# Third spectral stage of a fused spectral and gated kernel: spectrum as weights, the matrix over s1 streamed

## The chip, the cores and the metric

One core of one Trainium2 chip. The metric is device time in microseconds of one execution of the whole kernel. Three runs of the kernel before gave a median of 1438.85 us (1438.41 to 1439.46).

## What is computed

The reference, cut to what matters: one layer norm, then a sum of the input, a two-dimensional spectral filter and a gated block of two layers.

```python
B, S, D, F = 1, 2048, 576, 4608

def _A_ref(x, w_r, w_i):
    X = jnp.fft.rfft2(x, axes=(-2, -1))
    X = X * (w_r + 1j * w_i)
    return jnp.fft.irfft2(X, s=(S, D), axes=(-2, -1))

def _B_ref(x, w_gate, w_up, w_down):
    g = x @ w_gate
    u = x @ w_up
    return (sigmoid(g) * u) @ w_down

xn = layernorm(A_x)
out = A_x + _A_ref(xn, w_r, w_i) + _B_ref(xn, w_gate, w_up, w_down)
```

All numbers are float32. Matrix products run in float32r; where the precision asks for it an operand is split into a high part (rounded by a copy to float32r) and a low part (the difference), and a product becomes three: high by high, low by high, high by low.

## The kernel before

**The gated block** fills most of the time. The 2048 rows are taken in two halves (`PAIRS`), the inner dimension F in 36 blocks `f`; a unit `u` (function `unit`, helper `prod`, line 644) multiplies one block in seven block products of seven 128 x 512 matmuls each. These are the runs `pA`, `pB`, `pE` of seven matmuls. The way down is `down` (`po`, line 751) and, in the second half, `seven` (`ps`, line 842), which yields six matmuls of 288 columns for each pair of PSUM banks, and lets VectorE add each pair to `acc` or `qs` (line 852).

**The spectral filter** is computed beside the second half of the gated block. Rows are written as s = 32 s1 + s2; a product over s1 (64 values, real and imaginary parts stacked to 128) and one over s2 make the transform over the rows, and a matrix product over the 576 columns (folded to 288 by symmetry) makes the one over the columns. Three stages:

- `phase1b` (16 tiles): columns, then s1; its result goes to `sc1` in DRAM.
- `phase2` (16 blocks): s2, the multiplication by the filter, and s2 back (`pc`); the result `u`, two slices of 128 x 290, goes to `sc2` in DRAM with one copy by ScalarE (line 548) and one DMA.
- `phase3` (16 tiles): loads two slices of 128 x 290 from `sc2`, and the matrix over s1 `ai` (its high and low part for both slices); splits the spectrum into `uh` and `ul`; multiplies with `ai` as weights and the spectrum streamed (`py`, line 573, six matmuls of 290 columns); copies 256 of the 289 columns to `y` and splits the 33 left over into `rp` (high, low, high again); transposes both through TensorE (`pz`, lines 585 and 588, six transposes); splits the transposed result into `z3h`, `z3l` and the left-over rows `z3r`; multiplies by the matrix over the columns `dit` (`pe`, line 602, 14 matmuls of 288 columns); and adds the result to `acc` or to a spilled part of it (`fin`).

The spectral columns stand in the order of `KOF`: 256 columns, then 33 more (`FR` = 33, `REM` = 32), then one of zeros, which makes `NQ` = 290.

**The order of the work.** Each phase is a generator, started at a step of the main loop (`U1`, `U2`, `U3`: first step and steps between tiles; phase 3 starts at step 151 and every 4.5 steps). A step is one run of seven 512-column matmuls, then one piece of `seven` or `down`, then one piece (up to the next `yield`) of every active generator. Instructions of one engine run in the order in which the tile framework puts them; its scheduler may move a piece by some instructions, save those held by `keep_in_program_order`. All PSUM pairs (`pair`: `ps`, `po`, `py`, `pz`, `pe`, `pc` and others) share two buffers, so that each waits for the readers of the pair before the last. DMAs are issued by SyncE (SP) in one queue, with few exceptions at start and end. The rooms of the stages (`stage2`, `stage3`) hold the tiles of one stage each.

`split` writes the high part on ScalarE and the low part on VectorE:

```python
def split(hi, lo, src, eng=None):
    nc.scalar.activation(hi, src, AF.Copy)
    (eng or nc.vector).tensor_tensor(lo, src, f32(hi), op=OP.subtract)
```

Of the kernel before, what the change touches and what calls it, by code (L numbers as in the profile page):

```python
# [9 lines left out]
F32 = mybir.dt.float32  # L10
F32R = mybir.dt.float32r
I32 = mybir.dt.int32
AF = mybir.ActivationFunctionType
OP = mybir.AluOpType
PSUM = bass.MemoryType.PSUM

P = 128
S, D, F = 2048, 576, 4608
KD = D // 2 + 1
NQ = KD + 1  # L20
N1, N2 = 64, 32
NT = S // P
EPS = 1e-5
HD = D // 2
FR = HD + 1 - 2 * P
CW = 512
TPC = CW // P
PAIRS = S // (2 * CW)
TPP = 2 * TPC
KT = 2  # L30
REM = HD - KT * P
# [32 lines left out]
def _constants():  # L64
    out = {}

    mid = np.arange(HD) - (D - 1) / 2
    ang = 2 * np.pi * mid[:, None] * KOF[None, :] / D
    t = np.zeros((P, 2, 5, NQ), np.float32)
    for e, v in ((0, np.cos(ang)), (1, -np.sin(ang))):  # L70
        m = np.zeros((HD, NQ))
        m[:, :KD] = v
        m[:, KD - 1 if e == 0 else KT * P] = 0.0
        hi, lo = _split(m)
        for part, w in ((0, hi), (1, lo)):
            t[:, e, 2 * part] = w[:P]
            t[:, e, 2 * part + 1] = w[P:2 * P]
        t[:KR, e, 4] = np.concatenate([hi[2 * P:], hi[2 * P:], lo[2 * P:]])
    out["cf"] = t.reshape(P, 10 * NQ)


    s1 = np.arange(N1)
    k1 = np.arange(N1)
    am = np.zeros((P, N2, 2, P), np.float32)
    ai = np.zeros((P, N2, 2, P), np.float32)
    for s2 in range(N2):
        ph = 2 * np.pi * (((N2 * s1[:, None] + s2) * k1[None, :]) % S) / S
        m = _cplx(np.exp(-1j * ph))
        am[:, s2, 0], am[:, s2, 1] = _split(m)
        m = _cplx(np.exp(1j * ph).T)  # L90
        ai[:, s2, 0], ai[:, s2, 1] = _split(m)
    out["am"] = am.reshape(P, N2 * 2 * P)
    out["ai"] = ai.reshape(P, N2 * 2 * P)


    s2 = np.arange(N2)
    ph = 2 * np.pi * ((s2[:, None] * s2[None, :]) % N2) / N2
    bm = _cplx(np.kron(np.exp(-1j * ph), np.eye(2)))
    bi = _cplx(np.kron(np.exp(1j * ph), np.eye(2)))
    sca = np.arange(P).reshape(2, N2, 2).transpose(1, 0, 2).ravel()  # L100
    bm = bm[sca]
    bi = bi[:, sca]
    b = np.stack([*_split(bm), *_split(bi)], 1)
    out["bm"] = b.reshape(P, 4 * P)


    a = np.where((KOF == 0) | (KOF == HD), 1.0, 2.0)[:, None] / (D * S)
    co, si = a * np.cos(ang.T), a * np.sin(ang.T)
    co[KD - 1] = 0.0
    si[KT * P] = 0.0  # L110
    t = np.zeros((P, 2, 5, HD), np.float32)
    for e, m in ((0, co), (1, si)):
        hi, lo = _split(m)
        for part, w in ((0, hi), (1, lo)):
            t[:, e, 2 * part] = w[:P]
            t[:, e, 2 * part + 1] = w[P:2 * P]
        t[:3 * FR, e, 4] = np.concatenate([hi[2 * P:], hi[2 * P:], lo[2 * P:]])
    out["di"] = t.reshape(P, 10 * HD)
    out["id"] = np.eye(P, dtype=np.float32)
    return out  # L120
# [25 lines left out]
def spectral_glu_kernel(ctx: ExitStack, tc: tile.TileContext, x, ri, w_in, w_down, out):  # L146
    nc = tc.nc
    con = {k: nc.inline_tensor(v, name=f"c_{k}").ap() for k, v in _constants().items()}

    def f32(ap):  # L150
        return ap.bitcast(F32)
# [6 lines left out]
    def pair(name):  # L158
        return ps.tile([P, 2, 512], F32, tag="pp", name=name, bufs=2)

    fix = ctx.enter_context(tc.tile_pool(name="fix", bufs=1))
    idf = fix.tile([P, P], F32, name="idf")
    idr = fix.tile([P, P], F32R, name="idr")
# [15 lines left out]


    sc1 = tc.dram_tile([N2 * P, NQ], F32, name="sc1")
    sc2 = tc.dram_tile([N2 * P, NQ], F32, name="sc2")
    spill = tc.dram_tile([TPP * P, D], F32, name="spill")
    wsp = [tc.dram_tile([P, NX * 5 * P], F32, name=f"wsp{f}") for f in range(NF)]
    wdsp = [tc.dram_tile([P, 2 * D], F32, name=f"wdsp{f}") for f in range(NF)]
# [17 lines left out]
# [3 lines that stand above are left out]
# [305 lines left out]
    def phase2(i):  # L511
        pool, bm, zz = R["pool"], R["bm"], R["zz"]
        kl = 2 * i
        x2 = pool.tile([P, 2, NQ], F32, tag="x2", name=f"x2{i}", bufs=2)
        nc.sync.dma_start(x2, sc1.rearrange("(p kl) n -> p kl n", kl=N2)[:, kl:kl + 2])
        w = pool.tile([P, 2, 2, KD], F32, tag="ri", name=f"ri{i}", bufs=2)
        nc.sync.dma_start(w.rearrange("p a j n -> p (a j n)"), ri[i])
        wr, wi = w[:, 0], w[:, 1]
        yield
        yield  # L520
        yield
        h = pool.tile([P, 2, NQ], F32R, tag="x2h", name=f"x2h{i}")
        l = pool.tile([P, 2, NQ], F32R, tag="x2l", name=f"x2l{i}")
        tc.keep_in_program_order(nc.scalar.activation(h, x2, AF.Copy))
        nc.vector.tensor_tensor(l, x2, f32(h), op=OP.subtract)
        yield
        pb = pair(f"pb{i}")
        for j in range(2):
            for n, (k, m) in enumerate(((0, h), (0, l), (1, h))):
                nc.tensor.matmul(pb[:, j, :NQ], bm[:, k, :], m[:, j, :], start=n == 0, stop=n == 2)  # L530
        sw = pool.tile([P, 2, KD], F32, tag="sw", name=f"sw{i}")
        nc.scalar.activation(sw[:N1], pb[N1:, :, :KD], AF.Copy, scale=-1.0)
        nc.scalar.activation(sw[N1:], pb[:N1, :, :KD], AF.Copy)
        z = pool.tile([P, 2, KD], F32, tag="z", name=f"z{i}")
        t2 = pool.tile([P, 2, KD], F32, tag="t2", name=f"t2{i}")
        nc.vector.tensor_tensor(z, wr, pb[:, :, :KD], op=OP.mult)
        nc.vector.tensor_tensor(t2, wi, sw, op=OP.mult)
        nc.vector.tensor_tensor(z, z, t2, op=OP.add)
        zh, zl = zz[i % len(zz)]
        split(zh[:, :, :KD], zl[:, :, :KD], z)  # L540
        yield
        yield
        pc = pair(f"pc{i}")
        for j in range(2):
            for n, (k, m) in enumerate(((2, zh), (2, zl), (3, zh))):
                nc.tensor.matmul(pc[:, j, :NQ], bm[:, k, :], m[:, j, :], start=n == 0, stop=n == 2)  # L546
        u = pool.tile([P, 2, NQ], F32, tag="u", name=f"u{i}", bufs=2)
        nc.scalar.activation(u, pc[:, :, :NQ], AF.Copy)
        nc.sync.dma_start(sc2.rearrange("(p kl) n -> p kl n", kl=N2)[:, kl:kl + 2], u)

    def phase3(t):
        pool, di = R["pool"], R["di"]
        u = pool.tile([P, 2, NQ], F32, tag="u3", name=f"u3{t}", bufs=2)
        nc.sync.dma_start(u, sc2[2 * t * P:(2 * t + 2) * P].rearrange("(j p) n -> p j n", j=2))
        ai = pool.tile([P, 2, 2, P], F32R, tag="ai", name=f"ai{t}", bufs=2)
        load_r(ai, con["ai"][:, t * 4 * P:(t + 1) * 4 * P].rearrange("p (a h m) -> p a h m", a=2, h=2))
        if t < TPP:
            a = pool.tile([P, D], F32, tag="fin", name=f"fin{t}", bufs=2)
            nc.sync.dma_start(a, spill[t * P:(t + 1) * P, :])
        else:  # L560
            a = acc[t]
        yield
        yield
        yield
        uh = pool.tile([P, 2, NQ], F32R, tag="uh", name=f"uh{t}")
        ul = pool.tile([P, 2, NQ], F32R, tag="ul", name=f"ul{t}")
        tc.keep_in_program_order(nc.scalar.activation(uh, u, AF.Copy))
        nc.vector.tensor_tensor(ul, u, f32(uh), op=OP.subtract)
        yield
        py = pair(f"py{t}")  # L570
        for sl in range(2):
            for n, (h, m) in enumerate(((0, uh), (0, ul), (1, uh))):
                nc.tensor.matmul(py[:, sl, :NQ], ai[:, sl, h, :], m[:, sl, :], start=n == 0, stop=n == 2)  # L573
        y = pool.tile([P, 2, 2 * P], F32, tag="y", name=f"y{t}")
        nc.scalar.activation(y, py[:, :, :2 * P], AF.Copy)
        rp = pool.tile([P, 2, 3, FR], F32R, tag="rp3", name=f"rp3{t}")
        rem = py[:, :, 2 * P:KD]
        split(rp[:, :, 0, :], rp[:, :, 1, :], rem)
        nc.scalar.activation(rp[:, :, 2, :], rem, AF.Copy)
        yield  # L580
        pz = pair(f"pz{t}")
        for k in range(2):
            v = pz[:, 0, k * 256:(k + 1) * 256].rearrange("p (c a s) -> p c a s", c=2, a=2)
            for sl in range(2):
                nc.tensor.transpose(v[:, :, sl, :], y[:, sl, k * P:(k + 1) * P], idf)  # L585
        v = pz[:3 * FR, 1, :256].rearrange("p (c a s) -> p c a s", c=2, a=2)
        for sl in range(2):
            nc.tensor.transpose(v[:, :, sl, :].bitcast(F32R), rp[:, sl].rearrange("p a b -> p (a b)"), idr)
        zh = pool.tile([P, 2, 2, P], F32R, tag="z3h", name=f"z3h{t}")
        zl = pool.tile([P, 2, 2, P], F32R, tag="z3l", name=f"z3l{t}")  # L590
        zr = pool.tile([P, 2, P], F32R, tag="z3r", name=f"z3r{t}")
        split(zh, zl, pz[:, 0, :].rearrange("p (a c s) -> p a c s", a=2, c=2))
        nc.scalar.activation(zr[:3 * FR], pz[:3 * FR, 1, :256].rearrange("p (c s) -> p c s", c=2), AF.Copy)
        yield
        pe = pair(f"pe{t}")
        for e in range(2):
# [8 lines left out]
        lo, up = a[:, :HD], a[:, HD:]  # L605
# [414 lines left out]
    for p in range(PAIRS):  # L1020

        calls = [(0, 0), (1, 0), (0, 1), (1, 1)] if p == 0 else [(0, 0), (0, 1), (1, 0), (1, 1)]
        for n, (f, c) in enumerate(calls):
            u = p * NF + f
# [34 lines left out]
        for f in range(G, NF):  # L1059
            u = p * NF + f  # L1060
# [79 lines left out]
```

## Time and profile before

| | us |
|---|---|
| median of 3 runs | 1438.85 |
| profiled execution | 1438.32 |
| its span, first to last instruction | 1436.5 |
| third spectral stage, first `py` to last `pe` | 1184 to 1410 |
| second spectral stage | 960 to 1160 |

How to read the profile: PE is TensorE's matmuls, PEld its weight loads (which overlap matmuls), DVE is VectorE, ACT ScalarE, SP SyncE. Matmuls are pipelined and the ends of their records are modelled: the time that one occupies is read from start to start, or from the chain of work that ended last. That chain follows the work back from the last instruction, at each step to what released it or to the instruction before it on its engine; its pieces give start, length, and the number of instructions. A group of instructions has its line, engine, operation, output and inputs, shape (for a matmul: rows x weight columns, then rows x streamed columns), count, busy time, the mean of one in ns, and the engine's idle time before it with what ended it.

### The profile page before, as it was taken

Reading aid. Unit: us, or ns where it says so; the run is one execution under the profiler, and the core shown is the slowest. Engines: PE = TensorE matmul, PEld = TensorE weight load, DVE = VectorE, ACT = ScalarE, POOL = GpSimd, SP = SyncE. Lnnn points to the kernel's source line nnn. Section 1 sums busy time; section 2 is a strip of 40 time slices with the busy share of each in tenths; the row PEclk is TensorE's granted clock in tenths of the full one; section 3 lists DMA queues with packets and bytes.
Section 4 is the critical chain, followed back from the end, with each engine's and each line's share of the span. In section 5 each row is a group of like instructions: output and inputs, shape, how many; then the busy total and the mean of one; then the engine's idle time right before and its main releaser. Section 6 shows DMA issues by size and latency. Waiting matters only on the chain.

```text
span 1436.5 us, 21196 instructions
## 1 busy us (share of the span) xinstructions
PE 1422.8 (99%) x8073; PEld 1252.0 (87%) x8073; DVE 1087.7 (76%) x1734; ACT 653.5 (45%) x1122; POOL 3.3 (0%) x5
## 2 busy tenths in 40 slices
PE   8999999999999999999999999999999999999998
PEld 5888888888888888889888888888888889898997
DVE  7988888888888787766366687767888877766784
ACT  6644444444444444453345454434555534443431
POOL 0000000000000000000000000000000000000000
PEclk9999999999999999999999999999999999999999
DMA  7588677776777776655676766778888787776642
GB/s 247 195 329 313 256 274 264 265 264 255 262 255 271 262 276 232 230 215 181 213 215 204 210 201 207 206 220 269 273 270 269 245 282 243 226 227 195 202 125 83
DMA packets 128325, 338.79 MB, mean 236 GB/s; under 512 B 11872, under 2 KB 49248, under 8 KB 123360
## 3 DMA queue, kind: packets, MB, share of 16 engines
q1 hardware_dynamic: 127296, 336.13, 69.8%
q8 instruction: 64, 1.05, 0.3%
q10 hardware_dynamic: 928, 1.31, 0.2%
q14 instruction: 37, 0.30, 0.1%
HBM read 201.27 MB, written 136.12 MB: 235 GB/s over the span
## 4 chain that ended last, share of the span: by engine, by line
PE 97%; DVE 1%; ACT 1%; issue 0%; DMA 0%; ACTq 0%
PE pB L644 24%; PE po L751 19%; PE pE L644 16%; PE pA L644 16%; PE ps L842 12%; PE pe L602 2%; PE pd L494 2%; PE pc L546 1%; PE pa L506 1%; PE pb L530 1%; PE py L573 1%; PE pf L478 1%; PE pz L585 1%; PE b L900 0%; PE px_S L442 0%; PE px_A L442 0%
## 5 line engine op out<-in xcount | busy, mean ns | idle before, releaser
L644 PE MATMUL pB<-X,w 128*128 128x512 f32 x1484 | 382.4, 394 | 0.0
L644 PEld LDWEIGHTS pB<-X,w 128*128 128x128 f32 x1484 | 267.5, 188 | 49.5 <-ACT v L708 1.3
L644 PE MATMUL pE<-X,w 128*128 128x512 f32 x1064 | 273.1, 393 | 0.0
L644 PE MATMUL pA<-X,w 128*128 128x512 f32 x1008 | 259.7, 394 | 1.9 <-DVE X L448 1.2
L644 PEld LDWEIGHTS pE<-X,w 128*128 128x128 f32 x1064 | 192.8, 188 | 34.0
L644 PEld LDWEIGHTS pA<-X,w 128*128 128x128 f32 x1008 | 184.2, 189 | 35.8 <-DVE X L448 1.9
L751 PE MATMUL po<-wd,hh 128*128 128x288 f32 x1216 | 210.9, 295 | 0.0
L842 PEld LDWEIGHTS ps<-wf,hs 128*128 128x128 f32 x1260 | 188.6, 188 | 19.3 <-DVE qs L852 1.8
L842 PE MATMUL ps<-wf,hs 128*128 128x288 f32 x1260 | 204.2, 296 | 0.3 <-DVE qs L852 0.3
L751 PEld LDWEIGHTS po<-wd,hh 128*128 128x128 f32 x1216 | 184.4, 188 | 11.2
L755 DVE TENSOR_TENSOR acc<-acc,po 128x576 f32<-128x576 f32 x168 | 126.0, 750 | 76.7 <-PE po L751 75.5
L236 ACT ACTIVATE w<-raw 128x768 fp32r<-128x768 f32 (+1 forms) x106 | 100.8, 952 | 94.2 <-PE pE L644 37.9
L751 PE MATMUL po<-wd,hl 128*128 128x288 f32 x608 | 128.9, 293 | 0.0
L852 DVE TENSOR_TENSOR qs<-qs,ps 128x576 f32<-128x576 f32 x112 | 84.1, 751 | 31.1 <-PE ps L842 30.0
L751 PEld LDWEIGHTS po<-wd,hl 128*128 128x128 f32 x608 | 98.7, 189 | 0.0
L852 DVE TENSOR_TENSOR acc<-acc,ps 128x576 f32<-128x576 f32 x90 | 67.5, 750 | 24.2 <-PE ps L842 23.6
L238 DVE TENSOR_TENSOR w<-raw,w 128x512 fp32r<-128x512 f32 (+1 forms) x106 | 81.9, 773 | 3.2 <-ACT w L236 2.9
L729 DVE TENSOR_TENSOR y<-y,g 128x1024 f32<-128x1024 f32 x67 | 81.9, 1222 | 3.2
L709 DVE TENSOR_TENSOR y<-v,pE 128x512 f32<-128x512 f32 x68 | 46.7, 686 | 49.1 <-ACT v L708 48.2
L778 ACT ACTIVATE hs<-y 128x512 fp32r<-128x512 f32 x105 | 64.9, 629 | 38.9 <-DVE y L729 12.4
L712 ACT ACTIVATE g<-pB 128x512 f32<-128x512 f32 x68 | 40.7, 598 | 91.1 <-PE pB L644 91.1
L708 ACT ACTIVATE v<-pB 128x512 f32<-128x512 f32 x68 | 40.7, 598 | 71.9 <-PE pB L644 71.5
(165 smaller groups left out, 1667.9 us busy)
## 6 DMA issues: line engine op xcount, KB each, us to landing
w<-wsp SPq DMA_DIRECT2D x246, 320.0 KB, 3.5
wsp<-w SPq DMA_DIRECT2D x34, 2240.0 KB, 7.8
raw<-in_w SPq DMA_DIRECT2D x34, 768.0 KB, 9.7
wdsp<-wd SPq DMA_DIRECT2D x36, 576.0 KB, 4.6
wf<-tsp SPq DMA_DIRECT2D x60, 288.0 KB, 3.8
wf<-wdsp SPq DMA_DIRECT2D x45, 288.0 KB, 4.0
std<-in_wd SPq DMA_DIRECT2D x36, 288.0 KB, 5.4
ri<-in_ri SPq DMA_DIRECT2D x16, 578.0 KB, 5.3
```

The lines of the kernel that those rows point to most:

```text
L236: placed(nc.scalar.activation(o[:, :, :3, :], src, AF.Copy))
L238: placed(nc.vector.tensor_tensor(o[:, :, 3:, :], src[:, :, :KT, :], f32(o[:, :, :KT, :]), op=OP.subtract))
L644: nc.tensor.matmul(bank, w[:, sw, :], X[:, x, sx, :], start=start and j == 0, stop=stop and j == len(STEPS) - 1, skip_group_check=skip)
L708: nc.scalar.activation(v[:, 1], bank["B"], AF.Copy)
L709: nc.vector.tensor_tensor(y[:, 1], v[:, 1], bank["E"], op=OP.add)
L712: nc.scalar.activation(g[:, 1], bank["B"], AF.Sigmoid)
L729: nc.vector.tensor_tensor(y, y, g, op=OP.mult)
L751: nc.tensor.matmul(pd[:, b, :HD], h[i], w[k][b], start=g == 0 and n == 0, stop=g == G - 1 and n == 2)
L755: nc.vector.tensor_tensor(a, a, pd[:, :, :HD], op=OP.add)
L778: nc.scalar.activation(hs[:, 0], src, AF.Copy)
L842: nc.tensor.matmul(pd[:, i, :HD], h[:, a, m], w[:, b], start=q == 0, stop=q == 2)
L852: nc.vector.tensor_tensor(o, o, pd[:, :, :HD], op=OP.add)
```

## The change

Phase 3 swaps the roles of its first product: the spectrum (`uh`, `ul`) is loaded as weights, in column groups of 128, 128 and 99, and `ai` is streamed, 128 columns at a time. The product then has the spectral columns on its partitions, which is what `pz` held before, and `py`, `y`, `rp`, the six transposes and one `yield` go away. For the left-over columns, phase 2 writes them three times: `u` grows from 290 to `NU` = 288 + 2 x 32 + 3 = 355 columns (288, the 32 of the rest twice more, column 288 three times), with three copies on ScalarE instead of one. The last 99 of these are the third column group. After the copy of `zr` a VectorE subtraction turns its rows 64 to 96 into the low part, and the rows of `di` are put in the matching order.

```diff
+NU = HD + 2 * (HD - 2 * P) + 3
...
-        t[:3 * FR, e, 4] = np.concatenate([hi[2 * P:], hi[2 * P:], lo[2 * P:]])
+        t[:3 * FR, e, 4] = np.concatenate([hi[2 * P:HD], lo[2 * P:HD], hi[2 * P:], hi[HD:], lo[HD:]])
...
-    sc2 = tc.dram_tile([N2 * P, NQ], F32, name="sc2")
+    sc2 = tc.dram_tile([N2 * P, NU], F32, name="sc2")
...
-        u = pool.tile([P, 2, NQ], F32, tag="u", name=f"u{i}", bufs=2)
-        nc.scalar.activation(u, pc[:, :, :NQ], AF.Copy)
+        u = pool.tile([P, 2, NU], F32, tag="u", name=f"u{i}", bufs=2)
+        nc.scalar.activation(u[:, :, :HD], pc[:, :, :HD], AF.Copy)
+        nc.scalar.activation(u[:, :, HD:NU - 3].rearrange("p j (a n) -> p j a n", a=2),
+                             pc[:, :, 2 * P:HD].unsqueeze(2).to_broadcast([P, 2, 2, REM]), AF.Copy)
+        nc.scalar.activation(u[:, :, NU - 3:], pc[:, :, HD:KD].to_broadcast([P, 2, 3]), AF.Copy)
...
-        u = pool.tile([P, 2, NQ], F32, tag="u3", name=f"u3{t}", bufs=2)
+        u = pool.tile([P, 2, NU], F32, tag="u3", name=f"u3{t}", bufs=2)
...
-        uh = pool.tile([P, 2, NQ], F32R, tag="uh", name=f"uh{t}")
-        ul = pool.tile([P, 2, NQ], F32R, tag="ul", name=f"ul{t}")
+        uh = pool.tile([P, 2, NU], F32R, tag="uh", name=f"uh{t}")
+        ul = pool.tile([P, 2, NU], F32R, tag="ul", name=f"ul{t}")
...
-        py = pair(f"py{t}")
-        for sl in range(2):
-            for n, (h, m) in enumerate(((0, uh), (0, ul), (1, uh))):
-                nc.tensor.matmul(py[:, sl, :NQ], ai[:, sl, h, :], m[:, sl, :], start=n == 0, stop=n == 2)
-        y = pool.tile([P, 2, 2 * P], F32, tag="y", name=f"y{t}")
-        nc.scalar.activation(y, py[:, :, :2 * P], AF.Copy)
-        rp = pool.tile([P, 2, 3, FR], F32R, tag="rp3", name=f"rp3{t}")
-        rem = py[:, :, 2 * P:KD]
-        split(rp[:, :, 0, :], rp[:, :, 1, :], rem)
-        nc.scalar.activation(rp[:, :, 2, :], rem, AF.Copy)
-        yield
         pz = pair(f"pz{t}")
-        for k in range(2):
-            v = pz[:, 0, k * 256:(k + 1) * 256].rearrange("p (c a s) -> p c a s", c=2, a=2)
+        r = slice(2 * P, NU)
+        for o, c in [(pz[:, 0, k * 256:(k + 1) * 256], slice(k * P, (k + 1) * P)) for k in range(KT)] + [(pz[:3 * FR, 1, :256], r)]:
+            v = o.rearrange("p (c a s) -> p c a s", c=2, a=2)
             for sl in range(2):
-                nc.tensor.transpose(v[:, :, sl, :], y[:, sl, k * P:(k + 1) * P], idf)
-        v = pz[:3 * FR, 1, :256].rearrange("p (c a s) -> p c a s", c=2, a=2)
-        for sl in range(2):
-            nc.tensor.transpose(v[:, :, sl, :].bitcast(F32R), rp[:, sl].rearrange("p a b -> p (a b)"), idr)
+                for n, (h, m) in enumerate(((0, uh), (0, ul), (1, uh))):
+                    nc.tensor.matmul(v[:, :, sl, :], m[:, sl, c], ai[:, sl, h, :], start=n == 0, stop=n == 2)
...
-        nc.scalar.activation(zr[:3 * FR], pz[:3 * FR, 1, :256].rearrange("p (c s) -> p c s", c=2), AF.Copy)
+        v = pz[:3 * FR, 1, :256].rearrange("p (c s) -> p c s", c=2)
+        nc.scalar.activation(zr[:3 * FR], v, AF.Copy)
+        r = slice(2 * REM, 3 * REM + 1)
+        nc.vector.tensor_tensor(zr[r], v[r], f32(zr[r]), op=OP.subtract)
```

## The prediction

> **What bounds the kernel now.** I read the profile from the outside in: first the busy times of the whole span, then the busy time of each engine by stage, then the chain of work that ended last.
>
> ```profile
> span 1436.5 us, 21196 instructions
> PE 1422.8 (99%) x8073; PEld 1252.0 (87%) x8073; DVE 1087.7 (76%) x1734; ACT 653.5 (45%) x1122; POOL 3.3 (0%) x5
> ...
> PE 97%; DVE 1%; ACT 1%; issue 0%; DMA 0%; ACTq 0%
> ```
>
> TensorE (PE) is busy for nearly all of the span, and the chain runs over it for 97%. The third spectral stage lies between the first product `py` (1184 us) and the last `pe` (1410 us), the second between 960 and 1160 us. Busy time by stage (stretch; its length; PE, weight loads, DVE, ACT, POOL with counts; clock, DMA share, GB/s):
>
> ```profile
> 960.00:1160.00 200.00, 199.99 (x1119) 174.83 (x1118) 163.81 (x237) 100.38 (x166) 0.00 (x0) 1.00 0.83 264
> ...
> 1184.00:1410.00 226.00, 225.99 (x1357) 204.46 (x1356) 162.85 (x265) 92.66 (x194) 0.00 (x0) 1.00 0.65 195
> ```
>
> In both PE has no gap, at the full granted clock (PEclk 1.00). So in the stage that changes time is a sum of PE pieces: what the edit takes off VectorE (DVE) or ScalarE (ACT) is worth nothing by itself, and no PE idle time is left to win. What counts is what the exchanged matmuls occupy. The chain in order of time (start us, us, what) shows one tile of the stage and its neighbours:
>
> ```profile
> 1184.04 0.80 PE ps L842 x6
> 1184.83 0.81 PE py L573 x6
> 1185.64 1.60 PE pA L644 x7
> 1187.24 0.80 PE ps L842 x6
> 1188.04 0.44 PE pz L585 x4
> 1188.47 0.15 PE pz L588 x2
> 1188.62 1.68 PE pB L644 x7
> ```
>
> **What is removed on PE.** Per tile the six 290-column products `py` hold PE for 0.81 us and the six transposes `pz` for 0.44 + 0.15 = 0.59. The run of seven 512-column matmuls behind the transposes takes 1.68 instead of 1.60: 0.08 more, the short matmuls give the next weight load too little to hide behind. Together 0.81 + 0.59 + 0.08 = 1.48 us.
>
> **What is added on PE.** Three column groups (128, 128 and 99 columns of the spectrum as weights) times two slices times three terms: 18 matmuls, each with its own weight load and only 128 streamed columns. The trace has no ordinary float32r product that streams under 288 columns, so the price of one has to be bounded. Count columns alone and the change looks good: before 6 x 290 + 6 x 128 = 2508, after 18 x 128 = 2304. The rows say that columns don't set the pace of short matmuls. Matmuls by start, and weight loads by shape (busy us, mean ns):
>
> ```profile
> 1187.07 0.96 PE L842 MATMUL ps<-wf,hs 128*128 128x288 f32 x6
> 1187.87 0.60 PE L585 MATMUL pz<-idf,y 128*128 128x128 f32 x4
> 1188.23 0.40 PE L588 MATMUL pz<-idr,rp 128*99 128x128 f32 x2
> 1188.46 1.84 PE L644 MATMUL pB<-X,w 128*128 128x512 f32 x7
> ```
> ```profile
> L573 PEld LDWEIGHTS py<-uh,ai 128*128 128x128 f32 x64 | 11.2, 189 | 0.0
> L585 PEld LDWEIGHTS pz<-idf,y 128*128 128x128 f32 x64 | 7.8, 140 | 0.2 <-ACT rp L579 0.2
> L588 PEld LDWEIGHTS pz<-idr,rp 128*99 128x99 f32 x32 | 4.4, 166 | 0.0
> ```
>
> From start to start, four transposes take 1188.23 - 1187.87 = 0.36, 90 ns each, with loads of 140 ns; two with 99 weight columns take 0.23, 115 ns each, with loads of 166 ns; six ordinary products take 0.80, 133 ns each, with loads of 189 ns (288 or 290 columns streamed). The spacing is each time the load less 50 to 56 ns, though the first two stream the same 128 columns. I read this as the weight load setting the pace. An ordinary load of 128 columns is the 189 ns kind, so 12 of the new matmuls cost 133 ns; for the six with 99 weight columns I take the 115 ns of the other 99-column load. Sum: 12 x 0.133 + 6 x 0.115 = 2.29 us, and 0.08 for the run behind, as now: 2.37.
>
> Net per tile 2.37 - 1.48 = +0.89 us, over 16 tiles +14.2 us. Break-even lies at (1.48 - 0.08) / 18 = 78 ns for one matmul.
>
> Bounds of this price: below, the transposes' pace, 12 x 0.090 + 6 x 0.115 = 1.77, net +0.37, +5.9 us. Another stretch of transposes gives nearly the same (12 from 10.23 to 11.36 us, 94 ns each):
>
> ```profile
> 10.23 0.60 PE L442 MATMUL px_A<-idf,xa 128*128 128x128 f32 x4
> ...
> 11.36 0.44 PE L918 MATMUL b<-idr 128*128 128x512 f32 x1
> ```
>
> Above, a short product that needs four passes over its 128 columns would cost a 512-column one, 1.60 / 7 = 229 ns: 18 x 0.229 = 4.12, net +2.64, +42 us. I take the load's pace since it is the nearest row: same type, same kind of load, same stationary size.
>
> The Trainium skill speaks against the change too, but more softly: "TensorE: Matmul & The Clock Gate", section "LDWEIGHTS (loading the stationary operand)", puts a load at its column count over 1.2 GHz, which would make 107 and 82 ns here; by it the tile would be an estimated 12 x 0.107 + 6 x 0.082 + 0.08 - 1.48 = +0.38 us, +6 us in all. The trace has 133 ns with such loads, but streamed 288 columns beside them, so it doesn't refute the page.
>
> **ACT and DVE in stage 3.** Off ACT come the copy `y` and two small ones of `rp`, off DVE the `rp` subtraction; `uh` and `ul` grow from 580 to 710 elements. All of it lies beside PE, so I count nothing. One piece is new in a chain that PE does wait for: after `zr` a DVE subtraction of 33 x 256 from PSUM. `pe` gets the PSUM pair that `pz` held, and can't start before this last reader.
>
> ```profile
> 1188.66 0.60 ACT L204 ACTIVATE z3h<-pz 128x512 fp32r<-128x512 f32 x1 [0.79 <-DMA ai<-c_ai]
> 1189.29 0.69 DVE L205 TENSOR_TENSOR z3l<-pz,z3h 128x512 fp32r<-128x512 f32 x1 [0.46 <-DMA ai<-c_ai]
> 1190.02 0.39 ACT L593 ACTIVATE z3r<-pz 99x256 fp32r<-99x256 f32 x1 [0.76 <-DVE z3l L205]
> ...
> 1190.83 0.19 PEld L602 LDWEIGHTS pe<-dit,z3h 128*128 128x128 f32 x1
> ```
> ```profile
> L607 DVE TENSOR_TENSOR fin<-fin,pe 128x288 f32<-128x288 f32 x8 | 3.6, 446 | 0.0
> L205 DVE TENSOR_TENSOR rp<-py,rp 128x66 fp32r<-128x66 f32 x16 | 3.6, 226 | 5.3 <-ACT rp L204 5.0
> ```
>
> By the last two rows a column costs (446 - 226) / 222 = 1 ns, so 256 columns take about 415 ns. `z3r` ends at 1190.41, `pe` loads at 1190.83: the slack of 0.42 us is just used up. The order of instructions in the changed program puts 1 to 6 matmuls of the next run ahead of `pe` in 10 of 16 tiles (2 before), 0.23 us of cover each; in six it follows directly. There I take 0.1 us, together +0.5. With the cover gone in all tiles it is 16 x 0.45 = 7 us. While DVE waits for `zr`, the next sum of `ps` stands behind it, and its PSUM pair with it, which the second pair after it needs: covered by a run of seven (1.60 us). A divided run costs nothing by itself: 0.46 + 1.15 = 1.61 where it is divided now.
>
> ```profile
> 1289.24 0.46 PE pE L644 x2
> 1289.70 1.89 PE pe L602 x14
> 1291.59 1.15 PE pE L644 x5
> ```
>
> **Stage 2 and the DMAs.** Writing `u` becomes three ACT copies (576, 128 and 6 elements) instead of one (580).
>
> ```profile
> L548 ACT ACTIVATE u<-pc 128x580 f32<-128x580 f32 x16 | 10.5, 654 | 16.6 <-PE pc L546 16.3
> L842 PEld LDWEIGHTS ps<-wf,hs 128*128 128x128 f32 x480 | 72.0, 188 | 5.9 <-DVE z L536 0.3 <-ACT u L548 0.3
> L604 ACT ACTIVATE od<-pe 128x288 f32<-128x288 f32 x16 | 6.6, 411 | 32.0 <-PE pe L602 32.0
> L204 ACT ACTIVATE rp<-py 128x66 fp32r<-128x66 f32 x16 | 3.5, 222 | 0.0
> ```
>
> By the last two rows a copy is 166 ns plus 0.85 ns a column: 275 and 171 ns more, 0.45 us a block, 7.1 us of ACT in a window where ACT is busy 100 of 200 us. PE has waited for this copy for 0.3 us in all 16 blocks. I count nothing; were the whole 0.45 exposed, 7 us. The rows of `sc2` grow from 290 to 355 columns, and its DMAs with them:
>
> ```profile
> sc<-u SPq DMA_DIRECT2D x16, 290.0 KB, 3.8
> u<-sc SPq DMA_DIRECT2D x16, 290.0 KB, 4.5
> ```
>
> That is 32 x 65 KB = 2.1 MB more; if they land in proportion, 4.7 and 5.5 us. The load is issued three steps ahead, and a step is never under 1.60 + 0.80 us in the chain above, 7.2 us: hidden. No issue is moved past another queue's work on purpose; the loads of stage 3 stay in the same step, only its two products come one step earlier, and the last tile still ends inside the main loop.
>
> **Sum.** The profiled execution took 1438.32 us, 1.8 beside its span, 0.5 under the median of 1438.85. 1438.3 + 14.2 + 0.5 = 1453.0, on the median's scale 1453.5. I forecast 1454 us, about 1.0% slower, with 1449 to 1458 for this case by itself.
>
> **The rivals.** Times on the median's scale.
> - *The load's own pace is the transposes'*: the 189 ns are latency and loads follow each other every 90 ns. Then +5.9, 1445 us. For it: the recorded load is longer than any spacing. Against: 288 columns at 133 ns sit above the line that columns alone explain.
> - *Several passes*: short float32r products lose the single pass. Then +42, 1481 us. For it: nothing in the trace shows an ordinary product under 288 columns, all of this kernel's are wider. Against: the transposes stream 128 four-byte columns at 90 ns, not 229.
> - *The new wait decides*: +14.2 and 7 us more, 1460 us.
> - *No change*: one matmul at 68 to 88 ns, within 2.9 us of 1439 us. This needs loads to hide nearly wholly. The Trainium skill has a rule to this end: the same page, section "Back-to-back issue gap", gives some 81 ns for a 128-column pair of load and matmul in a stream; by that figure the time would be an estimated +1 us. No stretch of transposes here reaches it.
> - *Faster*: weight loads hide completely and columns alone set the pace. The line through 512 columns (229 ns) and 288 (133 ns) gives 0.43 ns a column and 64 ns at 128: 18 x 0.064 + 0.08 - 1.48 = -0.25, -4.0 us, 1435 us. It decides from 68 ns downward. For it: fewer columns, and 512 and 288 lie well on such a line. Against: the transposes, with lighter loads, are at 90 ns.
>
> **How the numbers follow.** Forecast 0.48, several passes 0.23, the transposes' pace 0.14, the new wait 0.05, no change 0.05, faster 0.05. The range reaches from the transposes' pace to the several passes, 1443 to 1482 us, and leaves 0.10 out. A measurement of this kernel can tell about 0.2%, 2.9 us, from no change; faster 0.05, same 0.05, slower 0.90.
>
> **What would show it.** The `pz` group has 18 matmuls a tile with weight loads of about 189 ns (166 for 99 columns) and takes 2.2 to 2.4 us in the chain; PE stays without gaps, and the stretch from the first `pz` to the last `pe` grows by about 14 us, while stages before it keep their length. Pieces of 1.6 us or 4 us, a gap in PE ahead of `pe` on the new subtraction, or a longer stage 2 on `u` would each point to one of the rivals. A `pz` group under 1.4 us makes the forecast wrong in sign.

## The result, and the profile after

The changed kernel takes 1457.74 us (median of 4 runs, 1454.95 to 1457.98) against 1438.78 before: ratio 1.0127, interval 1.0109 to 1.0144. It is 19 us slower; the forecast was 15.

The first lines of its page, and the third stage by windows (stretch; length; PE, weight loads, DVE, ACT, POOL; clock, DMA share, GB/s):

```profile
span 1456.1 us, 21347 instructions
PE 1435.2 (99%) x8169; PEld 1260.8 (87%) x8169; DVE 1094.6 (75%) x1734; ACT 644.9 (44%) x1106; POOL 3.3 (0%) x5
...
PE 94%; DVE 4%; ACT 1%; issue 0%; DMA 0%; ACTq 0%; DVEq 0%
```
```profile
960.00:1160.00 200.00, 199.99 (x1119) 175.31 (x1119) 164.77 (x238) 104.73 (x198) 0.00 (x0) 1.00 0.84 270
...
1185.70:1425.00 239.30, 231.60 (x1422) 207.28 (x1422) 167.68 (x261) 78.75 (x144) 0.00 (x0) 0.99 0.61 188
```

The second stage is as it was; the first `pz` comes at 1185.8 us, the first `py` came at 1184.8. The third stage has grown from 224 us (1184.8 to 1408.7) to 239, and what is new to it is 239.30 - 231.60 = 7.7 us in which PE stands still. (For the same work the growth is larger, 18.6 us: the last `pe` now stands one step earlier, so that one run of seven and one piece of `po`, 1.60 + 1.58 us, lie behind it that lay ahead of it before.) The chain, which ran over PE alone there, now leaves it for VectorE (4% of the whole span). One tile without such a gap, from the chain in order of time:

```profile
1185.02 0.80 PE ps L837 x6
1185.81 1.81 PE pz L580 x18
1187.63 1.67 PE pA L639 x7
```

The 18 matmuls hold PE for 1.81 us, the run behind them takes 1.67 instead of 1.60. Net per tile 1.81 + 0.07 - 1.48 = 0.40 us, 6.4 us over 16 tiles: a third of the loss, not all of it. The starts of the matmuls and their weight loads:

```profile
1186.49 0.39 PE L580 MATMUL pz<-ai,uh 128*128 128x128 f32 x2
1186.71 0.27 PE L580 MATMUL pz<-ai,ul 128*128 128x128 f32 x1
1186.83 0.36 PE L580 MATMUL pz<-ai,uh 128*128 128x128 f32 x2
1187.03 0.25 PE L580 MATMUL pz<-ai,ul 128*99 128x128 f32 x1
1187.12 0.34 PE L580 MATMUL pz<-ai,uh 128*99 128x128 f32 x2
1187.29 0.25 PE L580 MATMUL pz<-ai,ul 128*99 128x128 f32 x1
```
```profile
L580 PEld LDWEIGHTS pz<-ai,uh 128*128 128x128 f32 x128 | 20.6, 191 | 0.1
...
L580 PEld LDWEIGHTS pz<-ai,uh 128*99 128x99 f32 x64 | 9.5, 168 | 0.0
```

Two at `uh` in 0.22 us: 111 ns apiece with 128 weight columns. From 1187.03 to 1187.29 three: 87 ns with 99. A load is recorded with 191 and 168 ns, so the records of two loads overlap by some 80 ns. The four transposes of the kernel before went at the same pace. Their row in the prediction spans 0.60 us, and one of them lasts 273 ns, which leaves three spacings in 0.33 us, 109 ns each:

```profile
L585 PE MATMUL pz<-idf,y 128*128 128x128 f32 x64 | 9.7, 273 | 0.0
```

The rest sits ahead of `pe`. The group of its first matmuls, with the idle time before them, and the five instructions that carry that time:

```profile
L597 PE MATMUL pe<-dit,z3h 128*128 128x288 f32 x128 | 32.7, 313 | 7.7 <-DVE z3r L588 6.3 <-DVE acc L847 1.4
```
```profile
1207.44 0.38 PE L597 MATMUL pe<-dit,z3h 128*128 128x288 f32 x1 [2.30 <-DVE z3r L588]
1254.81 0.58 PE L597 MATMUL pe<-dit,z3h 128*128 128x288 f32 x1 [2.45 <-DVE z3r L588]
1358.61 0.37 PE L597 MATMUL pe<-dit,z3h 128*128 128x288 f32 x1 [0.59 <-DVE z3r L588]
1390.32 0.37 PE L597 MATMUL pe<-dit,z3h 128*128 128x288 f32 x1 [1.36 <-DVE acc L847]
1422.91 0.37 PE L597 MATMUL pe<-dit,z3h 128*128 128x288 f32 x1 [0.99 <-DVE z3r L588]
```

The long waits are in five tiles of 16, and they aren't the subtraction as such: it is late because all that it follows is late. The first of the five, ScalarE and VectorE by time:

```profile
1200.75 1.15 ACT L773 ACTIVATE hs<-y 128x512 fp32r<-128x512 f32 x2 [3.85 <-DVE y L724]
1203.55 0.63 ACT L773 ACTIVATE hs<-y 128x512 fp32r<-128x512 f32 x1 [1.65 <-DVE y L811]
1204.09 0.58 ACT L205 ACTIVATE z3h<-pz 128x512 fp32r<-128x512 f32 x1
...
1205.54 0.38 ACT L586 ACTIVATE z3r<-pz 99x256 fp32r<-99x256 f32 x1 [0.39 <-DVE z3l L206]
```
```profile
1204.82 0.68 DVE L206 TENSOR_TENSOR z3l<-pz,z3h 128x512 fp32r<-128x512 f32 x1
1205.42 1.41 DVE L811 TENSOR_TENSOR y<-y,y 128x512 f32<-128x512 f32 x2
1206.86 0.43 DVE L588 TENSOR_TENSOR z3r<-pz,z3r 33x256 fp32r<-33x256 f32 x1
```

The last `pz` ends at 1201.3. ScalarE is done with a pair of `hs` at 1201.9, is then idle for 1.65 us and doesn't touch `pz`: next in its queue stands another `hs`, a factor of the next round, which waits for VectorE's sums `y`. `z3h` starts at 1204.09, 2.8 us after its input. Two more sums stand ahead of the subtraction. The second of the five has the same order. In the other three it is other work that stands ahead of a reader: in the fourth, for one, VectorE does three sums before `z3l`, which starts 3.5 us after the last `pz`, and `pe` waits for a sum `acc` right behind it:

```profile
1384.77 4.14 DVE L856 TENSOR_TENSOR qs<-qs 128x1152 f32<-128x1152 f32 x3
```

A wait can cost more than its idle time. After the second one the granted clock is half for a while; the whole of `pe` falls in it and takes 1258.20 - 1254.81 = 3.39 us instead of 1.84:

```profile
1254.00:1258.00 4.00, 3.19 (x13) 3.22 (x14) 2.68 (x5) 0.03 (x1) 0.00 (x0) 0.58 0.29 91
```

Shorter waits don't show as idle time, since the record of a matmul runs on past the next start (512-column matmuls start every 0.23 us and are recorded with 0.39). They show in the length of `pe`. Here it is in a tile of the changed kernel without a gap, in the kernel before, and in the changed kernel without the subtraction (an experiment below):

```profile
1222.02 2.10 PE pe L597 x14
```
```profile
1204.03 1.86 PE pe L602 x14
```
```profile
1223.33 1.87 PE pe L595 x14
```

In the eleven tiles without a long wait `pe` takes 1.89 to 2.10 us, where the kernel before has 1.87 in nearly all; over the 16 tiles `pe` takes 3.8 us more, of which 1.6 are the half clock.

And 1 us lies ahead of all this. Early in the profiled execution the clock was lower for longer than in the one before (changed kernel first), and the first sum of `po` comes at 64.93 instead of 63.90 us:

```profile
14.00:23.00 9.00, 7.93 (x26) 5.82 (x27) 7.20 (x19) 4.42 (x10) 0.00 (x0) 0.62 0.38 147
```
```profile
14.00:23.00 9.00, 7.31 (x30) 5.40 (x29) 7.65 (x21) 3.80 (x9) 0.00 (x0) 0.81 0.50 180
```

The two profiled executions lie 19.6 us apart: 6.4 are the product, 7.7 idle time, 1.6 the half clock behind a wait, 2.2 the late starts of `pe` that show no idle time, and 1.0 the start of the execution. 0.7 us remain that can't be placed.

### The profile page after: what moved, and what is told of

Same layout as the page of the kernel before. It is cut to its first block, busy times and chain, and to the rows that moved or that the text cites. A ratio compares the mean times of both kernels' runs of the same rounds, so it can differ in the third digit from the quotient of the medians.

```text
span 1456.1 us, 21347 instructions
## 1 busy us (share of the span) xinstructions
PE 1435.2 (99%) x8169; PEld 1260.8 (87%) x8169; DVE 1094.6 (75%) x1734; ACT 644.9 (44%) x1106; POOL 3.3 (0%) x5
## 4 chain that ended last, share of the span: by engine, by line
PE 94%; DVE 4%; ACT 1%; issue 0%; DMA 0%; ACTq 0%; DVEq 0%
PE pB L639 23%; PE po L746 18%; PE pE L639 16%; PE pA L639 15%; PE ps L837 11%; PE pe L597 2%; PE pd L495 2%; PE pz L580 1%; PE pc L547 1%; PE pb L531 1%; PE pa L507 1%; PE pf L479 1%; PE b L895 0%; DVE hs L774 0%; PE px_S L443 0%
## 5 line engine op out<-in xcount | busy, mean ns | idle before, releaser
L774 DVE TENSOR_TENSOR hs<-y,hs 128x512 fp32r<-128x512 f32 x105 | 71.1, 686 | 3.9 <-ACT hs L773 3.3
```

The costliest lines, as they stand in the source:

```text
L774: return lambda: nc.vector.tensor_tensor(hs[:, 1], src, f32(hs[:, 0]), op=OP.subtract)
```

## The experiments

Two questions were open: whether the weight load or the columns set the price of the product, and what makes the readers of `pz` late. Four runs began it. Each has its own runs of the kernel before beside it.

**One step more between `pz` and `pe`.**

```diff
         nc.vector.tensor_tensor(zr[r], v[r], f32(zr[r]), op=OP.subtract)
         yield
+        yield
         pe = pair(f"pe{t}")
```

> Changed kernel with one more step between the product pz and pe, so that two runs of seven and two pieces of six lie between them (4.8 us instead of 2.4). Theory W (of the 19 us some 7 are the product itself, 18 matmuls at 1.81 us a tile against 1.40 us before plus the run behind, and some 12 are pe waiting for the last reader of pz): the long waits ahead of pe vanish, 1445 to 1448 us. Rival P (the waits only show a loss that lies elsewhere, in the product or the wider spectrum): 1455 to 1458 us, the gaps reappear ahead of ps.

1450.33 us, ratio 1.0084 (1.0069 to 1.0099). That is 7.4 us less than the changed kernel, between what theory W and rival P allowed. Waits of PE in the stage (engine, line, waited for: total, times, longest):

```profile
PE ps L838 <- DVE z3r L588: 3.6, 2, 2.1
PE ps L838 <- DVE acc L848: 0.8, 1, 0.8
```

`pe` no longer waits; three times `ps` does, which now takes the PSUM pair that `pz` held. The waits belong to the late readers, whoever comes next. That they cost a good part of the loss stood (7.4 us went with the step); that one more step takes them all away was wrong.

**Without the subtraction.**

```diff
         nc.scalar.activation(zr[:3 * FR], v, AF.Copy)
-        r = slice(2 * REM, 3 * REM + 1)
-        nc.vector.tensor_tensor(zr[r], v[r], f32(zr[r]), op=OP.subtract)
```

> Changed kernel without the VectorE subtraction on zr: the low part of the left-over columns is left out (its rows hold the high part again). Theory W with the subtraction as its cause: pe starts one VectorE instruction earlier, the waits shrink to about nothing as before the change, 1445 to 1448 us. Rival Q (the readers of pz come late because ScalarE and VectorE have other work queued ahead of z3h and z3l, whatever the last reader is): half of the waits stay, 1449 to 1453 us. Rival P: 1455 to 1458 us.

1455.84 us, 1.0117 (1.0100 to 1.0134): 1.9 us less than with it, which is no clear difference, since the intervals overlap.

```profile
PE pe L595 <- ACT z3r L586: 6.6, 4, 2.2
```

The long waits are nearly the same, only for `z3r` now: the subtraction isn't their cause. The time is not that of rival Q but in the range of rival P, as far more than half of the waits stayed. That the readers are late for work queued ahead of them, whatever the last reader is, is so far argued; the run with the order pinned, below, shows it. What the subtraction does cost shows in `pe`, which takes 1.87 us again in the tiles without a wait.

**Each product streamed in two halves.**

```diff
-                for n, (h, m) in enumerate(((0, uh), (0, ul), (1, uh))):
-                    nc.tensor.matmul(v[:, :, sl, :], m[:, sl, c], ai[:, sl, h, :], start=n == 0, stop=n == 2)
+                for q in range(2):
+                    for n, (h, m) in enumerate(((0, uh), (0, ul), (1, uh))):
+                        nc.tensor.matmul(v[:, q, sl, :], m[:, sl, c], ai[:, sl, h, q * N1:(q + 1) * N1], start=n == 0, stop=n == 2)
```

> Changed kernel with each of the 18 products streamed as two of 64 columns: the same columns, twice the weight loads. Theory L (the weight load sets the pace, column count over 1.2 GHz, 111 and 85 ns as the trace of the changed kernel has it): pz takes about 3.6 us a tile instead of 1.81, 16 x 1.8 = 29 us more, 1483 to 1490 us, spacing unchanged at 111 and 85 ns. Rival C (the columns set it, 128 columns plus a fixed part): spacing near 60 to 75 ns, pz 2.2 to 2.6 us, 6 to 13 us more.

1491.69 us, 1.0369 (1.0353 to 1.0384). The chain, and the stretch behind it by windows:

```profile
1184.39 3.65 PE pz L581 x36
1188.04 2.89 PE pA L640 x7
```
```profile
1184.80:1187.90 3.10, 3.10 (x33) 3.10 (x32) 0.39 (x1) 0.00 (x0) 0.00 (x0) 1.00 0.95 332
1187.90:1191.40 3.50, 3.50 (x12) 2.87 (x12) 2.01 (x3) 2.10 (x4) 0.00 (x0) 0.54 0.49 164
```

The same columns with twice the loads take twice the time: 3.65 us for 36, 101 ns on average, as 1.81 / 18 = 101 ns was. Half the streamed columns make nothing shorter. Nor is it a fixed price for each matmul, as the starts show:

```profile
1185.71 0.39 PE L581 MATMUL pz<-ai,uh 128*128 128x64 f32 x2
...
1186.38 0.39 PE L581 MATMUL pz<-ai,uh 128*128 128x64 f32 x2
...
1187.00 0.34 PE L581 MATMUL pz<-ai,uh 128*99 128x64 f32 x2
...
1187.53 0.34 PE L581 MATMUL pz<-ai,uh 128*99 128x64 f32 x2
```

Between the first two rows six matmuls start in 0.67 us, 112 ns each with 128 weight columns; between the last two six in 0.53 us, 88 ns each with 99. All stream 64 columns; the ratio is 0.79, that of the weight columns 0.77. So the load sets the pace. 16 x 1.84 = 29 us of the 34 above the changed kernel are this; the time came out 1.7 us above the range. The run of seven behind takes 2.89 us at a granted clock of 0.54, and so it goes nine times in the stage, for 3.4 or 6.8 us each. Against that, PE waits for only 0.8 us in this stage instead of 7.7.

**The subtraction alone, in the kernel before.** Its result goes to a scratch tile and isn't used.

```diff
         nc.scalar.activation(zr[:3 * FR], v, AF.Copy)
+        xs = pool.tile([P, 2, P], F32, tag="xs", name=f"xs{t}")
+        nc.vector.tensor_tensor(xs[r], v[r], f32(zr[r]), op=OP.subtract)
```

> Kernel before, with the changed kernel's subtraction added behind z3r into a scratch tile that nobody reads: the product is the old one, only pz gets a last reader 0.43 us later. Theory W: gaps ahead of pe appear where before were none, 2 to 9 us more, 1441 to 1448 us. Rival Q (the subtraction matters only with the new order of work): under 1 us more. In both PE has the old 1.40 us for py and pz.

1440.17 us beside 1438.52, 1.0010 (1.0001 to 1.0019): some 1.6 us, between the two forecasts and without a long gap ahead of `pe`. The sixteen `pe` together take 1.4 us more than in the kernel before (2.03 us in the tile at 1232.69, 1.87 before). The longer chain of readers costs that much by itself.

**The step of the main loop.** The next guess was that `pz`, which had moved one step ahead with the `yield` that went away, met the steps with the most other work.

```diff
+        yield
         pz = pair(f"pz{t}")
```

> Changed kernel with the yield that went away with py put back ahead of pz, so that pz and pe stand at the same steps of the main loop as before the change. Theory S (the waits come from the step: one step earlier pz meets the steps in which ScalarE and VectorE hold the gate product and the sums of the next round ahead of z3h): the gaps of 1 to 2.5 us vanish, what stays is the product's 6.8 us and about 1.7 us for the longer chain of readers, 1445 to 1448 us. Rival Q (the new reader chain loses against the queues wherever it stands): gaps elsewhere, 1451 to 1458 us.

1460.85 us, 1.0147 (1.0133 to 1.0161): slower still and above both forecasts, with five waits for `z3r`, 9.5 us. The same without the subtraction:

> As e5_yield_kept, and without the subtraction on zr (the low part of the left-over columns is left out). Theory S: only the product is left, 1445 to 1446 us, no gap ahead of pe. If the subtraction matters at these steps too, e5_yield_kept is 1 to 3 us above this run; if not, both agree within 1 us.

1454.78 us, 1.0116 (1.0097 to 1.0135), five waits again, 8.0 us. This is 6.1 us less than with the subtraction, where 1 to 3 were expected. Part of it is the clock: with the subtraction the granted clock fell to half behind two of the five waits, without it behind none. And the kernel before, begun one step earlier:

```diff
-U1, U2, U3 = (0, 4.1), (76, 4.1), (151, 4.5)
+U1, U2, U3 = (0, 4.1), (76, 4.1), (150, 4.5)
```

> Kernel before with the third stage begun one step earlier (150 instead of 151), so that its pz stands at the steps where the changed kernel has it; nothing else is changed. Theory S in its pure form (the step alone makes the readers of pz late): gaps ahead of pe like the changed kernel's, 1443 to 1450 us. Rival (the old order copes, since py and its small copies change what stands in the queues): within 1 us of 1438.5.

1440.19 us beside 1438.85, 1.0008 (0.9999 to 1.0017), a difference that can't be told from none, and no wait ahead of `pe`. Theory S falls on all three.

**The order in the queues.** What the five late tiles share is that a reader of `pz` stands behind other work in the order in which ScalarE's and VectorE's instructions were laid down; in the two with the longest waits it is `z3h` behind a factor copy `hs` that waits for a sum. In the second tile of the kernel before (`pz` done at 1201.6) `z3h` comes first and that `hs` after it:

```profile
1201.59 0.60 ACT L204 ACTIVATE z3h<-pz 128x512 fp32r<-128x512 f32 x1 [0.57 <-PE pz L588]
1202.52 0.63 ACT L778 ACTIVATE hs<-y 128x512 fp32r<-128x512 f32 x1 [0.34 <-DVE y L816]
```

First, program order alone: in the third stage a step gives out its spectral piece ahead of its piece of `ps` and the factors.

```diff
+                late = step >= U3[0]
-                if u > NF + G:
+                if u > NF + G and not late:
                     next(rounds, None)
...
                     aside()
+                    if late:
+                        next(rounds, None)
```

> Changed kernel, in whose third stage each step gives out the spectral piece ahead of the piece of ps and of the factors of the next round (program order alone; the scheduler may still move instructions). Theory O (what is left beside the product is z3h and z3l standing in the fixed queues behind the factor copies hs, which themselves wait for VectorE's sums): with z3h ahead of them in the tiles concerned the gaps of 2 to 3 us ahead of pe shrink to below 1 us, 1445 to 1450 us. Rival Q2 (ScalarE and VectorE lack the time in these steps, whatever the order): the gaps stay or move ahead of ps, 1453 to 1460 us.

1456.55 us, 1.0125 (1.0109 to 1.0140). The time is in rival Q2's range. The scheduler still put `hs` ahead in the same two tiles (`z3h` 1.1 us after `pz`, `z3l` 3.4 us after), and 5.3 us of waits stay, now mostly put down to a sum `acc`:

```profile
PE pe L597 <- DVE acc L847: 4.3, 3, 2.0
```

Since the order that the theory asks for wasn't reached, the run decides nothing, and the order was pinned:

```diff
+        i = nc.scalar.activation(hs[:, 0], src, AF.Copy)
+        if step > U3[0]:
+            tc.keep_in_program_order(i)
...
+            i = nc.vector.tensor_tensor(A[put], A[a], A[b], op=op)
+            if step > U3[0]:
+                tc.keep_in_program_order(i)
```

> As e9_readers_first, and in the third stage the factor copies hs on ScalarE and the factor sums on VectorE are held behind what was given out before them, so that z3h and z3r come first for sure. Theory O: no gap ahead of pe over 1 us, 1444 to 1448 us, that is the product's 7 us and little else. Rival Q2: 1453 us or more, with ps waiting for its factors instead.

1448.07 us beside 1438.30, 1.0070 (1.0053 to 1.0086): 9.7 us less than the changed kernel, or 9.2 less if each is taken against its own runs of the kernel before. Its stage by windows, and the second tile:

```profile
1185.50:1414.00 228.50, 228.38 (x1402) 202.50 (x1402) 166.45 (x262) 79.48 (x144) 0.00 (x0) 1.00 0.64 196
```
```profile
1199.36 0.60 ACT L205 ACTIVATE z3h<-pz 128x512 fp32r<-128x512 f32 x1 [2.68 <-PE pz L580]
1199.98 0.69 DVE L206 TENSOR_TENSOR z3l<-pz,z3h 128x512 fp32r<-128x512 f32 x1 [0.29 <-ACT z3h L205]
```

The last `pz` ends at 1199.26, `z3h` follows at once, PE has lost 0.1 us in the whole stage and its clock is full. Theory O stands, though for more than the `hs` that it named: the work is the same and both engines have the time; only the order differs. What is left, 9.8 us, is mostly the product, which with this order takes more in some tiles where it follows a 512-column run directly; in others it takes the 1.81 us that it had behind `ps`.

```profile
1195.63 1.60 PE pE L639 x7
1197.24 2.02 PE pz L580 x18
1199.26 0.83 PE ps L841 x6
...
1316.43 1.81 PE pz L580 x18
```

That is 2.02 + 0.03 - 1.48 = 0.57 us in six tiles and, by 1.81, about 0.36 in the other ten (five of these are divided): some 7 us. PE has no gap in the 3 us that are left; they aren't placed. The exchange of order alone, in the kernel before:

> Kernel before with the same exchange of order in its third stage as e9_readers_first. No theory has anything to win here, PE has no gap in this stage: within 1.5 us of before, 1437 to 1440 us. It shows what the exchange alone does.

1438.51 us beside 1438.30, 1.0003 (0.9993 to 1.0012): nothing. The pins weren't tried in the kernel before.

**Wider left-over columns.** In the kernel before, `rp` padded from 99 to 128 columns:

```diff
+        rq = pool.tile([P, 2, P], F32R, tag="rp3", name=f"rp3{t}")
+        nc.gpsimd.memset(f32(rq)[:, :, 3 * FR:], 0.0)
+        rp = rq[:, :, :3 * FR].rearrange("p s (a b) -> p s a b", a=3)
...
+            nc.tensor.transpose(v[:, :, sl, :].bitcast(F32R), rq[:, sl], idr)
```

> Kernel before with the left-over columns of the transposes padded from 99 to 128, 29 zeros set by GpSimd: the weight load of 99 columns took 166 ns, that of 128 only 140. If the row count of the load alone sets its pace, the two transposes get slower, 115 to 140 ns each; if loads in whole groups of 32 columns are the faster kind, they fall to about 90 ns, 0.05 us a tile, 0.8 us in all, 1437.7 us; either way within 1 us of before.

1438.43 us beside 1438.85, 0.9998 (0.9990 to 1.0007): no difference that can be told. The transposes and the run of seven behind them together take 2.25 us instead of 2.27, start to start. The record of the load did get shorter, from 166 ns to 141, with next to nothing gained:

```profile
L590 PEld LDWEIGHTS pz<-idr,rp 128*128 128x128 f32 x32 | 4.0, 141 | 0.0
```

No version beat the kernel before.

## Why the prediction was right, and where its terms were wrong

The time, the sign and the range held. That the time held was luck: the sum had two errors against each other, 8 us too much for the product and some 11 too little for what `pe` waits and what follows from it. Two of its own signs of being right failed: `pz` takes 1.81 us, not 2.2 to 2.4, and PE has gaps ahead of `pe`.

- *PE bounds the stage, nothing to win beside it*: right. Almost without waits (the order pinned) the kernel still loses 9.8 us, most of it what the product costs, though copies were taken off ScalarE and VectorE.
- *The weight load sets the pace of a short product*: right, and shown by the halved streams. Its size was wrong: I took 133 and 115 ns from products of 288 columns and from transposes, the runs have 111 and 87 ns; 1.81 us a tile where the sum had 2.29, 6.4 us with the run behind where it had 14.2. The wrong inference was that 133 ns at 288 columns was the load's own pace, and it rested on a misread row. The 90 ns of the four transposes count the short step of 0.03 us to the next kind of transpose as a fourth spacing; among themselves they lie 109 ns apart. So loads recorded with 140 and with 191 ns both follow each other every 109 to 111 ns, and "the load less 50 to 56 ns" is no rule. The rule of the Trainium skill ("TensorE: Matmul & The Clock Gate", section "LDWEIGHTS (loading the stationary operand)": column count over 1.2 GHz) gave 107 and 82 ns, an estimated 1.78 us a tile; the measured 1.81 agrees with it within 2%, and the single spacings of 111 and 87 ns lie 4 and 6% above it.
- *The new reader of `pz`*: the term of 0.5 us. I saw the chain with its 0.42 us of slack rightly, but priced it with ScalarE and VectorE free, as in the one tile that I read. In five tiles the readers stood behind other work in fixed queues; order alone is worth 9 to 10 us (the run with the order pinned). The subtraction's own part, which is what the 0.5 us were for, is some 1.6 us in the kernel before, and 6.1 us at the steps of the run with the `yield` put back, where the clock fell as well. The place, the sign (a gap ahead of `pe`) and nearly the time were those of the rival "the new wait decides", 1460 us; but its sum had 14.2 us for the product and 7 for the wait, and its mechanism was the lost cover, not the order in the queues.
- *A moved piece*: I costed the removed `yield` at nothing. Putting it back changed which tiles are late and made the kernel 3 us slower, so it wasn't what the loss came from.
- *Stage 2 and the DMAs*: right. ScalarE is busy 104.7 instead of 100.4 us there, PE 199.99 as before; the wider DMAs land in 3.9 and 4.4 us, sooner than the 4.7 and 5.5 by proportion.
- *Divided runs cost nothing*: right; a run around `pe` takes 0.47 + 1.14 = 1.61 us in the changed kernel.
- *The rivals*: several passes is out (101 ns on average, 229 needed). Faster and no change are out by the price above the break-even of 78 ns. The transposes' pace, 1.77 us a tile, came near the product's 1.81, though from the misread 90 ns, and was wrong about the total.

## What to carry to other kernels

Count weight loads, not columns, when a product is turned so that few columns are streamed: here 18 loads at 111 or 87 ns replaced 6 products at 133 ns and 6 transposes that took 0.59 us together, though fewer columns went through. Read a spacing inside one group of equal matmuls, not across its end. When PE is full, every reader of a PSUM buffer that PE will take again is on the path; its price is read from what stands ahead of it in its engine's queue in every tile, not from its own length in one. Before a change is judged by its time, look whether the scheduler laid down another order: half of this loss was order and came back with an exchange of order and two pins.

## What the runs showed of the hardware that wasn't expected

- The granted clock fell to half without any idle time. In the run with halved streams 3.65 us of short matmuls kept PE busy throughout, and the next 3.5 us had a clock of 0.54; a run of seven took 2.89 us instead of 1.60. It fell nine times in that stage, in which PE waited only once, for 0.8 us. In the changed kernel it fell once in the stage, after a wait of 2.45 us; a wait of 2.30 us there, and one of 2.45 us with the `yield` put back, were followed by no fall.
- Loads of 128 weight columns follow each other every 109 to 112 ns whether their records last 140 ns (transposes) or 191 (products), and with 128 or 64 streamed columns.
- The record of a weight load of 128 columns is shorter than that of one of 99 in a transpose: 141 against 166 ns, and 96 columns were at 126. In the new product the 99-column load has the shorter record, 168 against 191 ns.
